# Nyström attention into a mixture of experts on one core: swapped matmul operands, batched copies and a bfloat16 bridge transposed by DMA

## The chip, the cores and the metric

The kernel runs on one core of a Trainium2 chip. The metric is the device time of one execution in microseconds (us), from the profiler's clock. Engines are named as in the profile: PE is TensorE's matmul stream and PEld its weight loads, DVE is VectorE, ACT is ScalarE, POOL is GpSimd, and SP is SyncE, whose queue issues every DMA of this kernel. A tensor in SBUF or PSUM lies on up to 128 partitions.

## The reference, cut to what matters

Attention runs on 64 heads (8 batches by 8 heads) of 576 tokens with 64 features. Means over 18 tokens give 32 landmarks for q and for k. The output is A · Z · C · v, with Z from six steps of a Newton iteration. Its result, read as 4608 tokens of 512 features, goes through a mixture of 8 experts with one expert for each token.

```python
q_lm = q.reshape(B, H, m, S // m, D).mean(axis=3)      # m = 32
k_lm = k.reshape(B, H, m, S // m, D).mean(axis=3)
A = sm(q, k_lm); Bm = sm(q_lm, k_lm); C = sm(q_lm, k)  # softmax of the scaled product
Z = Bm.T / (norm1(Bm) * norminf(Bm) + 1e-06)
for _ in range(6):
    Z = 2 * Z - Z @ Bm @ Z
attn = A @ Z @ C @ v
x = attn.transpose(0, 2, 1, 3).reshape(B * S, H * D)   # 4608 x 512
e_idx = argmax(x @ w_gate); gate_w = softmax(x @ w_gate)[e_idx]; eom = sigmoid(x @ w_output_gate)
out[mask] = gate_w[mask] * eom[mask, e] * (relu(x[mask] @ w1[e]) @ w2[e])
```

## The kernel before, in words

**Attention (L76 to L186).** One unrolled pass for each of the 64 heads. A head's 576 tokens are cut into five chunks, four of 128 and one of 64. The chunks of v, q and k come in by 15 DMAs. PE transposes each q chunk and each k chunk into a PSUM tile `pT` (L90, L96) and DVE copies each out on its own (L91, L97) into `qT` and `kT`, which have the features on partitions. The k chunks are loaded into the buffer of the q chunks, `qS`. Two reductions on DVE give the landmarks `qlmT` (L101) and `klmT` (L103).

The landmark matrix `Bm` is a small matmul (`pBm`, L107), an exponential with its row sum (L110) and a scaling (L112). Its largest column sum comes from a matmul with ones (`pcs`, L115) and a short chain on DVE into `c_bc` (L117 to L119).

The C side is computed with landmarks on partitions: `pC` (L129), 32 by 576, has `qlmT` as the stationary operand and streams `kT`. ACT takes the exponential and the row sums (L131, L135). Then five small transposes `pCT` (L144), five copies `CT` (L146) and five accumulating matmuls `pCv` (L147) give C · v, scaled by the reciprocal row sum at L152.

The Newton chain carries Z · Bm and Z · C · v side by side in one 32 by 96 tile: a first matmul `pWV` (L155), a scaling (L158), and six times a matmul (L161) and a DVE instruction (L162), each of which waits for the one before.

The A side has tokens on partitions. For each of the five chunks there are a matmul `pA` (L169), an exponential with row sum (L172), a reciprocal (L174), a scaling (L175), a transpose `pAT` (L178), a copy `AT` (L180), a matmul `pO` (L182) with the Newton result as the stationary operand, a copy `Ot` (L184) and a DMA into the bridge tensor (L185).

**The bridge.** The attention output lies in DRAM as `x_bridge`, float32, 512 features by 4608 tokens. Four DMAs of 2.36 MB bring it back (`stg`, L203) and four DVE casts (L204) make `xT` in bfloat16, with 128 features on partitions for each of four feature blocks. The DMA of the last block needs the last two heads of every batch.

**The experts (L206 to L305).** A router over 36 token tiles (`plog`, L218, then small DVE work and an exponential and a sigmoid on ACT, L227 and L236), then eight experts of bfloat16 matmuls `ph` (L258) and `py` (L266), then the output.

The kernel is written against a scheduler that places each instruction in its engine's queue when the program is built: an instruction that has its inputs takes a free engine, the one written earlier first. On the chip each queue runs in that order and waits on semaphores. Buffers of a tag are shared in turn: the SBUF tags of attention have two buffers, the PSUM tags one.

Of the kernel before, what the change touches and what calls it, by code (L numbers as in the profile page):

```python
# [34 lines left out]
def kernel(  # L35
# [11 lines left out]
    nc = tc.nc  # L47
    B, H, S, D = q.shape
# [3 lines left out]
    N = B * S  # L52
# [1 line left out]
    E = moe_w_gate.shape[1]  # L54
    F = moe_w1.shape[2]

    x_dram = nc.dram_tensor("x_bridge", (HD, N), F32, kind="Internal").ap()

    with tc.tile_pool(name="attn_const", bufs=1) as cpool, \
         tc.tile_pool(name="attn_sb", bufs=2) as sb, \  # L60
# [13 lines left out]
        while off < S:  # L74
            cp = min(128, S - off)
            tokchunks.append((off, cp))  # L76
            off += cp

        for b in range(B):
            for h in range(H):  # L80
                qT = sb.tile([64, S], F32, tag="qT")
                kT = sb.tile([64, S], F32, tag="kT")
                vS = sb.tile([128, len(tokchunks), 64], F32, tag="vS")
                qS = sb.tile([128, len(tokchunks), 64], F32, tag="qS")
                for ci, (o, cp) in enumerate(tokchunks):
                    nc.sync.dma_start(out=vS[:cp, ci, :], in_=v[b, h, o:o + cp, :])
                    nc.sync.dma_start(out=qS[:cp, ci, :], in_=q[b, h, o:o + cp, :])
                for ci, (o, cp) in enumerate(tokchunks):
                    pT = ps.tile([64, 128], F32, tag="pC")
                    nc.tensor.transpose(pT[:, :cp], in_=qS[:cp, ci, :], identity=I128[:cp, :cp])  # L90
                    nc.vector.tensor_copy(qT[:, o:o + cp], pT[:, :cp])  # L91
                for ci, (o, cp) in enumerate(tokchunks):
                    nc.sync.dma_start(out=qS[:cp, ci, :], in_=k[b, h, o:o + cp, :])
                for ci, (o, cp) in enumerate(tokchunks):
                    pT = ps.tile([64, 128], F32, tag="pC")
                    nc.tensor.transpose(pT[:, :cp], in_=qS[:cp, ci, :], identity=I128[:cp, :cp])  # L96
                    nc.vector.tensor_copy(kT[:, o:o + cp], pT[:, :cp])  # L97
# [23 lines left out]
                Cexp = sb.tile([32, S], F32, tag="Cexp")  # L121
                cs = sb.tile([32, 1], F32, tag="cs")
                cs2 = sb.tile([32, 1], F32, tag="cs2")
                off0 = 0
                first = True
                while off0 < S:
                    w = min(512, S - off0)
                    pC = ps.tile([32, 512], F32, tag="pC")
                    nc.tensor.matmul(pC[:, :w], lhsT=qlmT, rhs=kT[:, off0:off0 + w])  # L129
                    if first:  # L130
                        nc.scalar.activation(out=Cexp[:, off0:off0 + w], in_=pC[:, :w],  # L131
                                             func=EXP, scale=s_c, accum_out=cs)
                        first = False
                    else:
                        nc.scalar.activation(out=Cexp[:, off0:off0 + w], in_=pC[:, :w],  # L135
                                             func=EXP, scale=s_c, accum_out=cs2)
                        nc.vector.tensor_tensor(cs, cs, cs2, op=ADD)
                    off0 += w
                nc.vector.reciprocal(cs, cs)

                pCv = ps.tile([32, 64], F32, tag="pCv")
                for ci, (o, cp) in enumerate(tokchunks):
                    pCT = ps.tile([128, 32], F32, tag="pCT")
                    nc.tensor.transpose(pCT[:cp, :], in_=Cexp[:, o:o + cp], identity=I32)  # L144
                    CT = sb.tile([128, 32], F32, tag="CT")
                    nc.vector.tensor_copy(CT[:cp, :], pCT[:cp, :])  # L146
                    nc.tensor.matmul(pCv, lhsT=CT[:cp, :], rhs=vS[:cp, ci, :],  # L147
                                     start=(ci == 0), stop=(ci == len(tokchunks) - 1))
# [3 lines left out]
                nc.vector.tensor_scalar(out=BmCv[:, 32:96], in0=pCv, scalar1=cs, scalar2=None, op0=MUL)  # L152

                pWV = ps.tile([32, 96], F32, tag="pCv")
                nc.tensor.matmul(pWV, lhsT=Bm, rhs=BmCv)  # L155
                WV = sb.tile([32, 96], F32, tag="WV")
                WV2 = sb.tile([32, 96], F32, tag="WV2")
                nc.vector.tensor_scalar(out=WV, in0=pWV, scalar1=c_bc, scalar2=None, op0=MUL)  # L158
                cur, nxt = WV, WV2
                for _ in range(6):  # L160
                    nc.tensor.matmul(pWV, lhsT=cur[:, :32], rhs=cur)  # L161
# [3 lines left out]
                ZCv = cur[:, 32:96]  # L165

                for ci, (o, cp) in enumerate(tokchunks):
                    pA = ps.tile([128, 32], F32, tag="pA")
                    nc.tensor.matmul(pA[:cp, :], lhsT=qT[:, o:o + cp], rhs=klmT)  # L169
                    Aexp = sb.tile([128, 32], F32, tag="Aexp")  # L170
                    asr = sb.tile([128, 1], F32, tag="asr")
                    nc.scalar.activation(out=Aexp[:cp, :], in_=pA[:cp, :], func=EXP,  # L172
                                         scale=s_a, accum_out=asr[:cp, :])
                    nc.vector.reciprocal(asr[:cp, :], asr[:cp, :])  # L174
                    nc.vector.tensor_scalar(out=Aexp[:cp, :], in0=Aexp[:cp, :],  # L175
                                            scalar1=asr[:cp, :], scalar2=None, op0=MUL)
                    pAT = ps.tile([32, 128], F32, tag="pAT")
                    nc.tensor.transpose(pAT[:, :cp], in_=Aexp[:cp, :], identity=I128[:cp, :cp])  # L178
                    AT = sb.tile([32, 128], F32, tag="AT")
                    nc.vector.tensor_copy(AT[:, :cp], pAT[:, :cp])  # L180
                    pO = ps.tile([64, 128], F32, tag="pO")
                    nc.tensor.matmul(pO[:, :cp], lhsT=ZCv, rhs=AT[:, :cp])  # L182
                    Ot = sb.tile([64, 128], F32, tag="Ot")
                    nc.vector.tensor_copy(Ot[:, :cp], pO[:, :cp])  # L184
                    nc.sync.dma_start(out=x_dram[h * D:(h + 1) * D, b * S + o: b * S + o + cp],  # L185
                                      in_=Ot[:, :cp])  # L186

    TN = 128
    ntiles = N // TN
# [4 lines left out]
    with tc.tile_pool(name="moe_const", bufs=1) as mc, \  # L194
# [2 lines left out]
         tc.tile_pool(name="moe_sb", bufs=2) as msb, \  # L197
         tc.tile_pool(name="moe_ps", bufs=2, space=bass.MemoryType.PSUM) as mps:

        xT = xtp.tile([128, DCH, N], BF16)  # L200
        for dc in range(DCH):
            stg = msb.tile([128, N], F32, tag="stage")
            nc.sync.dma_start(out=stg, in_=x_dram[dc * 128:(dc + 1) * 128, :])  # L203
            nc.vector.tensor_copy(xT[:, dc, :], stg)  # L204

        wg = mc.tile([128, DCH, 2 * E], F32)  # L206
        nc.sync.dma_start(out=wg[:, :, :E], in_=moe_w_gate.rearrange("(dc d) e -> d dc e", d=128))
# [102 lines left out]
```

## Time and profile before

| | |
|---|---|
| time, median of 4 runs | 2439.44 us (2439.1 to 2439.86) |
| the profiled execution, its own time | 2439.67 us |
| its span, first to last instruction | 2437.9 us, 1.8 us less |
| granted TensorE clock, mean | 1.000 |
| PE, PEld busy | 2247.5 us (92%), 1046.3 us (43%) |
| DVE, ACT busy | 1163.6 us (48%), 619.4 us (25%) |
| attention, about | 0 to 1303 us |
| bridge and router, about | 1303 to 1434 us |
| experts and output, about | 1434 to 2438 us |

Busy time counts an engine's instructions alone. A float32 matmul shows as two instructions, each with its own weight load; a transpose shows as one. Since matmuls overlap in the pipeline, the time that one adds to a stream is read from the starts along the chain of waits and not from its duration.

### The profile page before, as it was taken

To read this page: it belongs to the slowest core of one execution; us is meant where nothing else is said; L and a number is where in the kernel's file an instruction comes from. 1 tells how busy PE (TensorE), PEld (TensorE's weight loads), DVE (VectorE), ACT (ScalarE), POOL (GpSimd) and SP (SyncE) were. 2 spreads that over 40 slices of the span, in tenths; PEclk is the share of its full clock that TensorE was granted. 3 is DMA by queue.
4 is the path that set the end of the run, shared out by engine and by line. 5 is a ranking of instruction groups with operands and counts; after the bars stand their busy time and mean duration, and the time that the engine had idled before them with its cause. 6 is when DMAs were issued, how large, how long until landed. Compare 5 with 4: busy or idle time off the path is not lost.

```text
span 2437.9 us, 27936 instructions
## 1 busy us (share of the span) xinstructions
PE 2247.5 (92%) x9267; PEld 1046.3 (43%) x9360; DVE 1163.6 (48%) x4278; ACT 619.4 (25%) x1780; POOL 0.7 (0%) x6
## 2 busy tenths in 40 slices
PE   7999999999999999999993049999999999999999
PEld 3444444444444444444441024444444444444444
DVE  4555555555555555555555422344444535444344
ACT  1111111111111111111113963333333333333333
POOL 0000000000000000000000000000000000000000
PEclk9999999999999999999999999999999999999999
DMA  1111111111111111111225200101010102000012
GB/s 34 31 30 30 30 30 31 31 30 30 31 31 30 30 30 30 30 31 30 66 65 205 85 0 1 70 1 69 1 69 1 69 1 69 1 1 1 1 75 82
DMA packets 171055, 92.08 MB, mean 38 GB/s; under 512 B 137120, under 2 KB 153504, under 8 KB 170400
## 3 DMA queue, kind: packets, MB, share of 16 engines
q1 hardware_dynamic: 170912, 90.30, 12.7%
q8 instruction: 75, 1.23, 0.2%
q14 instruction: 68, 0.56, 0.1%
HBM read 71.34 MB, written 18.87 MB: 37 GB/s over the span
## 4 chain that ended last, share of the span: by engine, by line
PE 86%; DVE 6%; ACT 4%; DMA 2%; issue 1%; SPq 0%; DVEq 0%; ACTq 0%
PE ph L258 20%; PE py L266 20%; PE pO L182 8%; PE pA L169 7%; PE pWV L161 6%; PE pC L129 6%; PE pCv L147 5%; PE pAT L178 4%; PE pCT L144 3%; PE pT L90 3%; PE pT L96 3%; DVE qlmT L101 2%; ACT L236 1%; ACT L227 1%; DVE WV L162 1%; PE pWV L155 1%
## 5 line engine op out<-in xcount | busy, mean ns | idle before, releaser
L258 PE MATMUL ph<-xT,w1b 128*128 128x512 bf16 x2257 | 513.2, 381 | 15.4 <-ACT hT L261 12.6
L261 ACT ACTIVATE hT<-ph 128x512 bf16<-128x512 f32 x576 | 343.7, 597 | 649.7 <-PE ph L258 628.0
L266 PE MATMUL py<-w2b,hT 128*128 128x512 bf16 x2258 | 506.1, 379 | 2.4
L274 DVE TENSOR_SCALAR ysc<-py,coeff 128x512 f32<-128x512 f32 x252 | 189.1, 751 | 451.2 <-PE py L266 434.2
L258 PEld LDWEIGHTS <-w1b 128*128 128x128 bf16 x2304 | 225.7, 98 | 293.6 <-issue 28.7
L266 PEld LDWEIGHTS <-hT 128*128 128x128 bf16 x2304 | 225.4, 98 | 271.8
L161 PE MATMUL pWV<-WV 32*32 32x96 f32 x768 | 200.8, 362 | 30.7 <-DVE WV L162 20.8
L182 PE MATMUL pO<-AT,WV 32*64 32x128 f32 (+1 forms) x640 | 204.9, 421 | 7.1 <-DVE Ot L184 1.3
L172 ACT ACTIVATE Aexp<-pA 128x32 f32<-128x32 f32 (+1 forms) x320 | 62.0, 194 | 518.4 <-PE pAT L178 464.0
L169 PE MATMUL pA<-klmT,qT 64*128 64x32 f32 (+1 forms) x640 | 188.4, 386 | 1.3 <-ACT Aexp L172 0.7
L131 ACT ACTIVATE Cexp<-pC 32x512 f32<-32x512 f32 x64 | 37.5, 586 | 582.4 <-PE pC L129 582.4
L276 DVE TENSOR_TENSOR ytot<-ytot,ysc 128x512 f32<-128x512 f32 x252 | 174.3, 692 | 8.5
L169 PEld LDWEIGHTS pA<-klmT,qT 64*128 64x128 f32 (+1 forms) x640 | 145.5, 286 | 36.8 <-ACT Aexp L172 16.3
L129 PE MATMUL pC<-kT,qlmT 64*32 64x512 f32 (+1 forms) x256 | 149.1, 684 | 0.4 <-DVE kT L97 0.3
L147 PE MATMUL pCv<-vS,CT 128*32 128x64 f32 (+1 forms) x640 | 134.6, 314 | 5.7 <-DVE CT L146 5.7
L146 DVE COPY CT<-pCT 128x32 f32<-128x32 f32 (+1 forms) x320 | 60.1, 188 | 165.4 <-PE pCT L144 165.1
L184 DVE COPY Ot<-pO 64x128 f32<-64x128 f32 (+1 forms) x320 | 83.9, 262 | 106.7 <-PE pO L182 106.2
L90 PE MATMUL pT<-I,qS 128*64 128x128 f32 (+1 forms) x320 | 127.6, 399 | 7.5 <-DMA qS<-in_q_dram 4.9
L96 PE MATMUL pT<-I,qS 128*64 128x128 f32 (+1 forms) x320 | 127.7, 399 | 5.5 <-DMA qS<-in_k_dram 3.9
L182 PEld LDWEIGHTS pO<-AT,WV 32*64 32x64 f32 x640 | 90.5, 199 | 93.5 <-DVE klmT L103 36.6
L162 DVE SCALAR_TENSOR_TENSOR WV<-WV,pWV 32x96 f32<-32x96 f32 x384 | 92.4, 241 | 77.3 <-PE pWV L161 72.8
L161 PEld LDWEIGHTS pWV<-WV 32*32 32x32 f32 x768 | 67.9, 136 | 132.0 <-DVE WV L162 100.1
(66 smaller groups left out, 1541.6 us busy)
## 6 DMA issues: line engine op xcount, KB each, us to landing
w1f<-in_moe_w_dram SPq DMA_DIRECT2D x8, 2048.0 KB, 7.8
w2f<-in_moe_w_dram SPq DMA_DIRECT2D x8, 2048.0 KB, 9.3
stg<-x_bridge SPq DMA_DIRECT2D x4, 2304.0 KB, 9.0
out_dram<-ytot SPq DMA_DIRECT2D x36, 256.0 KB, 2.0
vS<-in_v_dram SPq DMA_DIRECT2D x256, 32.0 KB, 1.9
qS<-in_q_dram SPq DMA_DIRECT2D x256, 32.0 KB, 1.9
qS<-in_k_dram SPq DMA_DIRECT2D x256, 32.0 KB, 1.7
x_bridge<-Ot SPq DMA_DIRECT2D x256, 32.0 KB, 1.8
```

The costliest lines, as they stand in the source:

```text
L90: nc.tensor.transpose(pT[:, :cp], in_=qS[:cp, ci, :], identity=I128[:cp, :cp])
L96: nc.tensor.transpose(pT[:, :cp], in_=qS[:cp, ci, :], identity=I128[:cp, :cp])
L129: nc.tensor.matmul(pC[:, :w], lhsT=qlmT, rhs=kT[:, off0:off0 + w])
L147: nc.tensor.matmul(pCv, lhsT=CT[:cp, :], rhs=vS[:cp, ci, :], start=(ci == 0), stop=(ci == len(tokchunks) - 1))
L161: nc.tensor.matmul(pWV, lhsT=cur[:, :32], rhs=cur)
L169: nc.tensor.matmul(pA[:cp, :], lhsT=qT[:, o:o + cp], rhs=klmT)
L182: nc.tensor.matmul(pO[:, :cp], lhsT=ZCv, rhs=AT[:, :cp])
L258: nc.tensor.matmul(ph, lhsT=w1b[:, dc, fc * 128:(fc + 1) * 128], rhs=xT[:, dc, t0 * TN:t0 * TN + ntk], start=(dc == 0), stop=(dc == DCH - 1))
L261: nc.scalar.activation(out=hT[:, fc, :], in_=ph, func=RELU)
L266: nc.tensor.matmul(py, lhsT=hT[:, fc, tt * TN:(tt + 1) * TN], rhs=w2b[:, fc, :], start=(fc == 0), stop=(fc == FCH - 1))
L274: nc.vector.tensor_scalar(out=ysc, in0=py, scalar1=coeff[:, t, e:e + 1], scalar2=None, op0=MUL)
L276: nc.vector.tensor_tensor(ytot[:, t, :], ytot[:, t, :], ysc, op=ADD)
```

## The change

**Bridge tensor.** `x_bridge` becomes bfloat16, 4608 tokens by 512 features. Each head writes its five chunks as 128 (or 64) tokens of 64 features, 128 bytes for each token. `xT` is allocated ahead of attention and is filled by four DMAs that transpose on the way. The float32 staging and its casts are gone. Two one-column copies out of the last block of `xT` into the two buffers of the tag `stage` stand ahead of the weight loads that use that tag.

**Transposes.** Four chunks are transposed into one PSUM tile of 64 by 512 and copied out at once, the fifth on its own; `pT` has two buffers. k has a buffer `kS` of its own. Edges in program order place the first six transposes of a head (its five of q and the first of k) behind the six Newton matmuls of the head before, one behind each.

**C side.** `pCe` has tokens on partitions: five matmuls with a chunk of `kT` as the stationary operand and `qlmT` streamed, then two exponentials. The transposes `pCT` and the copies `CT` are gone. v has a 65th column of ones, so that `pCv` gives the row sums too.

**A side.** `pAe` has landmarks on partitions: `klmT` is the stationary operand and `qT` is streamed, 512 and 64 columns, with an exponential behind each. `pO2` has a chunk of `AexpT` as the stationary operand and streams the Newton result with a column of ones, so that the division by the row sum comes at the end, on the whole tile. The transposes `pAT` and copies `AT` are gone.

```diff
-    x_dram = nc.dram_tensor("x_bridge", (HD, N), F32, kind="Internal").ap()
+    x_dram = nc.dram_tensor("x_bridge", (N, HD), BF16, kind="Internal").ap()
+    xtp0 = ctx.enter_context(tc.tile_pool(name="xt_early", bufs=1))
+    xT = xtp0.tile([128, HD // 128, N], BF16)
...
+        steps = []
         for b in range(B):
             for h in range(H):
+                prev, steps, nt = steps, [], 0
-                vS = sb.tile([128, len(tokchunks), 64], F32, tag="vS")
+                vSx = sb.tile([128, len(tokchunks), 65], F32, tag="vSx")
+                nc.vector.memset(vSx[:, :, 64:65], 1.0)
+                kS = sb.tile([128, len(tokchunks), 64], F32, tag="kS")
...
+                for c0, c1, w in ((0, 4, 512), (4, 5, 64)):
+                    pT = ps.tile([64, 512], F32, tag="pT", bufs=2)
+                    for ci in range(c0, c1):
+                        o, cp = tokchunks[ci]
+                        tr = nc.tensor.transpose(pT[:, o - c0 * 128:o - c0 * 128 + cp], in_=qS[:cp, ci, :], identity=I128[:cp, :cp])
+                        if prev and 0 <= nt - 0 < 6:
+                            tc.add_manual_dep(tr.ins, prev[nt - 0].ins.name, mybir.DependencyInfo(
+                                mybir.DependencyClass.NoSync, mybir.DependencyReason.DATA), reason="fill the Newton gap")
+                        nt += 1
+                    nc.vector.tensor_copy(qT[:, c0 * 128:c0 * 128 + w], pT[:, :w])
...
-                    pC = ps.tile([32, 512], F32, tag="pC")
-                    nc.tensor.matmul(pC[:, :w], lhsT=qlmT, rhs=kT[:, off0:off0 + w])
...
-                    nc.tensor.transpose(pCT[:cp, :], in_=Cexp[:, o:o + cp], identity=I32)
-                    nc.vector.tensor_copy(CT[:cp, :], pCT[:cp, :])
-                    nc.tensor.matmul(pCv, lhsT=CT[:cp, :], rhs=vS[:cp, ci, :],
...
+                for ci, (o, cp) in enumerate(tokchunks):
+                    nc.tensor.matmul(pCe[:cp, ci * 32:ci * 32 + 32], lhsT=kT[:, o:o + cp], rhs=qlmT)
+                nc.scalar.activation(out=CexpT[:, :128], in_=pCe[:, :128], func=EXP, scale=s_c)
+                nc.scalar.activation(out=CexpT[:64, 128:160], in_=pCe[:64, 128:160], func=EXP, scale=s_c)
+                for ci, (o, cp) in enumerate(tokchunks):
+                    nc.tensor.matmul(pCv, lhsT=CexpT[:cp, ci * 32:ci * 32 + 32], rhs=vSx[:cp, ci, :],
+                                     start=(ci == 0), stop=(ci == len(tokchunks) - 1))
                 cs = sb.tile([32, 1], F32, tag="cs")
+                nc.vector.reciprocal(cs, pCv[:, 64:65])
...
+                    steps.append(nc.tensor.matmul(pWV, lhsT=cur[:, :32], rhs=cur))
...
+                nc.vector.tensor_copy(ZCvx[:, :64], cur[:, 32:96])
+                nc.vector.memset(ZCvx[:, 64:65], 1.0)
+                AexpT = sb.tile([32, S], F32, tag="AexpT")
+                for o, w in ((0, 512), (512, S - 512)):
+                    pAe = ps.tile([32, 512], F32, tag="pAe")
+                    nc.tensor.matmul(pAe[:, :w], lhsT=klmT, rhs=qT[:, o:o + w])
+                    nc.scalar.activation(out=AexpT[:, o:o + w], in_=pAe[:, :w], func=EXP, scale=s_a)
+                pO2 = ps.tile([128, len(tokchunks), 65], F32, tag="pO2")
+                for ci, (o, cp) in enumerate(tokchunks):
+                    nc.tensor.matmul(pO2[:cp, ci, :], lhsT=AexpT[:, o:o + cp], rhs=ZCvx)
+                rinv = sb.tile([128, len(tokchunks), 1], F32, tag="rinv")
+                Ot = sb.tile([128, len(tokchunks), 64], BF16, tag="Ot")
+                for n, c0, c1 in ((128, 0, 4), (64, 4, 5)):
+                    nc.vector.reciprocal(rinv[:n, c0:c1, :], pO2[:n, c0:c1, 64:65])
+                    nc.vector.tensor_tensor(Ot[:n, c0:c1, :], pO2[:n, c0:c1, :64],
+                                            rinv[:n, c0:c1, :].to_broadcast([n, c1 - c0, 64]), op=MUL)
+                for ci, (o, cp) in enumerate(tokchunks):
+                    nc.sync.dma_start(out=x_dram[b * S + o: b * S + o + cp, h * D:(h + 1) * D],
+                                      in_=Ot[:cp, ci, :])
...
-        xT = xtp.tile([128, DCH, N], BF16)
         for dc in range(DCH):
-            stg = msb.tile([128, N], F32, tag="stage")
-            nc.sync.dma_start(out=stg, in_=x_dram[dc * 128:(dc + 1) * 128, :])
-            nc.vector.tensor_copy(xT[:, dc, :], stg)
+            nc.sync.dma_start(out=xT[:, dc, :], in_=x_dram[:, dc * 128:(dc + 1) * 128],
+                              transpose=True)
+        for _ in range(2):
+            hold = msb.tile([128, N], F32, tag="stage")
+            nc.vector.tensor_copy(hold[:, :1], xT[:, DCH - 1, :1])
```

The k transposes are written like the q transposes, out of `kS` into `kT`, and count `nt` on from 5.

## Rows read from the trace of the kernel before

**Rows 1.** Busy time by stretch: us, PE, PEld, DVE, ACT, POOL, clock, DMA share, GB/s.

```profile
300.00:600.00 300.00, 290.15 (x1080) 137.77 (x1080) 160.04 (x795) 38.73 (x240) 0.00 (x0) 1.00 0.13 30
...
1350.00:1400.00 50.00, 4.07 (x64) 2.95 (x64) 19.74 (x144) 49.08 (x81) 0.00 (x0) 1.00 0.11 42
...
1500.00:2000.00 500.00, 497.54 (x2265) 225.84 (x2310) 211.99 (x278) 171.94 (x288) 0.00 (x0) 1.00 0.09 34
```

**Rows 2.** The scaling L158, once a head: duration ns min/median/max, first and last start.

```profile
L158 DVE TENSOR_SCALAR WV<-pWV,c_bc x64: 299/305/306, 25.6 to 1290.1; 32x96 f32<-32x96 f32 x64
```

**Rows 3.** The chain of waits, 611 to 620 us: start us, us, what.

```profile
611.20 0.51 PE pWV L161 x2
611.71 0.35 PE pT L96
...
613.78 0.33 PE pAT L178
614.11 0.24 PE pT L96
614.35 0.61 PE pO L182 x2
...
615.17 1.84 PE pC L129 x2
...
617.12 0.56 PE pA L169 x2
...
618.29 0.35 PE pC L129 x2
618.64 0.24 PE pCT L144
...
619.44 0.35 PE pCv L147 x2
```

**Rows 4.** The chain of waits from the last head's Newton steps to the first expert.

```profile
1292.75 0.25 DVE WV L162
...
1293.05 0.54 PE pWV L161 x2
...
1301.84 1.70 DMA x_bridge<-Ot
...
1308.72 11.91 DMA stg<-x_bridge
...
1323.24 9.93 DMA w2f<-in_moe_w_dram
...
1433.77 0.49 ACT hT L261
```

**Rows 5.** ACT lines, 1270 to 1450 us: count, busy us, mean ns, idle before.

```profile
L236 ACT ACT_TABLE_LOAD x36 | 46.2, 1283 | 0.6
L227 ACT ACT_TABLE_LOAD x35 | 44.9, 1283 | 0.6
```

**Rows 6.** Lines by form, 300 to 600 us: busy us, mean ns, idle before, releasers.

```profile
L97 DVE COPY kT<-pT 64x128 f32<-64x128 f32 x60 | 16.7, 279 | 4.4
...
L131 ACT ACTIVATE Cexp<-pC 32x512 f32<-32x512 f32 x15 | 8.8, 586 | 136.9 <-PE pC L129 136.9
...
L152 DVE TENSOR_SCALAR BmCv<-pCv,cs 32x64 f32<-32x64 f32 x15 | 4.1, 272 | 7.5 <-PE pCv L147 6.8
...
L97 DVE COPY kT<-pT 64x64 f32<-64x64 f32 x15 | 3.2, 212 | 0.0
```

**Rows 7.** DMA: queue packets, MB, share of 16 engines; an issue with KB and landing us.

```profile
q1 hardware_dynamic: 170912, 90.30, 12.7%
...
stg<-x_bridge SPq DMA_DIRECT2D x4, 2304.0 KB, 9.0
```

**Rows 8.** The first head on the timeline: v and k loads, last k transpose.

```profile
7.78 0.43 SPq L86 DMA_DIRECT2D vS<-in_v_dram  x1
...
14.28 0.31 PE L96 MATMUL pT<-I,qS 64*64 64x64 f32 x1 [0.38 <-DVE kT L97]
```

More of the change, by code (lines that the diff above doesn't have):

```diff
@@ L85 @@
                 for ci, (o, cp) in enumerate(tokchunks):
-                    nc.sync.dma_start(out=vS[:cp, ci, :], in_=v[b, h, o:o + cp, :])
+                    nc.sync.dma_start(out=vSx[:cp, ci, :64], in_=v[b, h, o:o + cp, :])
                     nc.sync.dma_start(out=qS[:cp, ci, :], in_=q[b, h, o:o + cp, :])
-                for ci, (o, cp) in enumerate(tokchunks):
-                    pT = ps.tile([64, 128], F32, tag="pC")
-                    nc.tensor.transpose(pT[:, :cp], in_=qS[:cp, ci, :], identity=I128[:cp, :cp])
-                    nc.vector.tensor_copy(qT[:, o:o + cp], pT[:, :cp])
@@ L92 @@
[L92 to L97, printed above, removed]
+                for c0, c1, w in ((0, 4, 512), (4, 5, 64)):
[8 more added lines that the diff above has]
+                    nc.vector.tensor_copy(qT[:, c0 * 128:c0 * 128 + w], pT[:, :w])
@@ new lines @@
+                for ci, (o, cp) in enumerate(tokchunks):
+                    nc.sync.dma_start(out=kS[:cp, ci, :], in_=k[b, h, o:o + cp, :])
+                for c0, c1, w in ((0, 4, 512), (4, 5, 64)):
+                    pT = ps.tile([64, 512], F32, tag="pT", bufs=2)
+                    for ci in range(c0, c1):
+                        o, cp = tokchunks[ci]
+                        tr = nc.tensor.transpose(pT[:, o - c0 * 128:o - c0 * 128 + cp], in_=kS[:cp, ci, :], identity=I128[:cp, :cp])
+                        if prev and 0 <= nt - 0 < 6:
+                            tc.add_manual_dep(tr.ins, prev[nt - 0].ins.name, mybir.DependencyInfo(
+                                mybir.DependencyClass.NoSync, mybir.DependencyReason.DATA), reason="fill the Newton gap")
+                        nt += 1
+                    nc.vector.tensor_copy(kT[:, c0 * 128:c0 * 128 + w], pT[:, :w])
@@ L119 @@
                 nc.vector.reciprocal(c_bc, c_bc)
-                Cexp = sb.tile([32, S], F32, tag="Cexp")
-                cs = sb.tile([32, 1], F32, tag="cs")
[L123 to L127, printed above, removed]
-                    pC = ps.tile([32, 512], F32, tag="pC")
-                    nc.tensor.matmul(pC[:, :w], lhsT=qlmT, rhs=kT[:, off0:off0 + w])
[L130 to L143, printed above, removed]
-                    nc.tensor.transpose(pCT[:cp, :], in_=Cexp[:, o:o + cp], identity=I32)
-                    CT = sb.tile([128, 32], F32, tag="CT")
-                    nc.vector.tensor_copy(CT[:cp, :], pCT[:cp, :])
-                    nc.tensor.matmul(pCv, lhsT=CT[:cp, :], rhs=vS[:cp, ci, :],
-                                     start=(ci == 0), stop=(ci == len(tokchunks) - 1))
+                pCv = ps.tile([32, 65], F32, tag="pCv")
@@ new lines @@
+                pCe = ps.tile([128, 160], F32, tag="pCe")
+                CexpT = sb.tile([128, 160], F32, tag="CexpT")
+                for ci, (o, cp) in enumerate(tokchunks):
[5 more added lines that the diff above has]
+                                     start=(ci == 0), stop=(ci == len(tokchunks) - 1))
@@ L150 @@
+                cs = sb.tile([32, 1], F32, tag="cs")
+                nc.vector.reciprocal(cs, pCv[:, 64:65])
                 BmCv = sb.tile([32, 96], F32, tag="BmCv")
                 nc.vector.tensor_copy(BmCv[:, :32], Bm)
-                nc.vector.tensor_scalar(out=BmCv[:, 32:96], in0=pCv, scalar1=cs, scalar2=None, op0=MUL)
-                pWV = ps.tile([32, 96], F32, tag="pCv")
+                nc.vector.tensor_scalar(out=BmCv[:, 32:96], in0=pCv[:, :64], scalar1=cs, scalar2=None, op0=MUL)
@@ L155 @@
+                pWV = ps.tile([32, 96], F32, tag="pWV")
                 nc.tensor.matmul(pWV, lhsT=Bm, rhs=BmCv)
@@ L160 @@
                 for _ in range(6):
-                    nc.tensor.matmul(pWV, lhsT=cur[:, :32], rhs=cur)
+                    steps.append(nc.tensor.matmul(pWV, lhsT=cur[:, :32], rhs=cur))
                     nc.vector.scalar_tensor_tensor(out=nxt, in0=cur, scalar=2.0, in1=pWV,
@@ L164 @@
                     cur, nxt = nxt, cur
-                ZCv = cur[:, 32:96]
-                for ci, (o, cp) in enumerate(tokchunks):
[L168 to L186, printed above, removed]
@@ new lines @@
+                ZCvx = sb.tile([32, 65], F32, tag="ZCvx")
+                nc.vector.tensor_copy(ZCvx[:, :64], cur[:, 32:96])
[5 more added lines that the diff above has]
+                    nc.scalar.activation(out=AexpT[:, o:o + w], in_=pAe[:, :w], func=EXP, scale=s_a)
```

## The prediction, made before the changed kernel ran

> **What bounds the kernel now.** I read the table of stretches first. In attention PE is busy for 290 of 300 us, in the experts for 497.5 of 500, and in the router for 4 of 50, where ACT has 49 [rows 1]. The change touches only attention and the bridge, so the reader should look at what PE is busy with there. The granted clock is 1.00 in all three stretches, the router with its idle PE included; I count no change of clock.
>
> The scaling L158 runs once a head and gives the period: (1290.1 − 25.6)/63 = 20.07 us [rows 2]. Next is the chain of waits. It runs almost wholly through PE, matmul after matmul with no gap, apart from the Newton steps, where PE and DVE alternate [rows 3, 4]. So a head costs what its matmuls occupy of PE, and a little idle.
>
> The same chain at the end of attention gives the bridge: the last write lands at 1303.5, the last staging DMA and the last cast follow, and the router can start at 1323.2 [rows 4]. From there to the first expert at 1433.8 ACT swaps function tables, 71 loads of 1.28 us, 91 of 110 us [rows 4, 5]. The change leaves that as it is, and the experts behind it.
>
> **Pricing PE.** Starts along the chain give the time that an instruction adds. One of pC occupies 1.84/2 = 0.92 us for 32 stationary and 512 streamed columns, one of pA 0.56/2 = 0.28 for 128 and 32 [rows 3]. The line through the two is 1.667 ns for each column, loaded or streamed, plus 13 ns. It gives 0.333 for a transpose (64 and 128; the row has 0.35) and 0.173 for one of pCv (32 and 64; 0.175) [rows 3]. So a loaded column costs as much as a streamed one, which matters because the change swaps the operands. The Trainium skill says otherwise (TensorE: Matmul & The Clock Gate, Step-by-step: what each phase is for): the next tile's weights load while the present matmul runs. pA disagrees, since its 32 streamed columns alone would take 0.07 us and not 0.28.
>
> **PE's work, by head.** Removed:
> - pC 1.84 + 0.35 = 2.19, and pCT 4 × 0.24 + 0.17 = 1.13
> - pA 4 × 0.56 + 0.35 = 2.59 (the last chunk by the line)
> - pAT 4 × 0.33 + 0.17 = 1.49, and pO 4 × 0.61 + 0.45 = 2.89 (last chunks by the line)
>
> That is 10.29 us. Added:
> - pCe, with pA's shape: 2.59
> - pAe, with pC's shape: 2.19
> - pO2, 128 loaded and 65 streamed columns: 2 × 0.335 = 0.67, the last chunk 0.46, together 3.14
>
> That is 7.92. Kept: ten transposes 8 × 0.35 + 2 × 0.24 = 3.28, pCv 1.75 (the 65th column adds 2 ns), the two small matmuls 0.24 each by the line, and seven of pWV at 2 × 0.226. Sum 8.68. PE's work falls from 18.97 to 16.60 us. Before, 20.07 − 18.97 = 1.10 us of a period were idle.
>
> **The chain through a period.** PE won't be as full as before, since the edges tie the transposes to the Newton steps and less work is left to fill the waits. I follow one period from the end of a head's sixth Newton matmul:
> - PE takes two k transposes (0.70) while DVE does the last Newton instruction (0.25) and the copy of the result (about 0.2, as the 64-wide copy in [rows 6]).
> - pO2 of the old head then has its input and was written earlier, so it goes first: 3.84. Three k transposes: 4.78.
> - The batched copy. 128 columns take 279 ns and 64 take 212 [rows 6], so 512 take about 0.68. It starts behind the fourth transpose at 4.54 and ends at 5.26; PE has nothing to do for 0.5 us.
> - pCe with the two small matmuls slipped in, 3.07: 8.37. The reduction for klmT and the chains for Bm and c_bc lie beside it on DVE and ACT.
> - The exponential, under the 0.59 us of a 512-wide one [rows 6], about 0.3. pAe is the only thing ready and can't be interrupted: 10.2.
> - pCv: 11.96. Reciprocal, scaling (0.27, [rows 6]) and handovers 0.5, first pWV 0.54, scaling 0.3 (its row, [rows 2]): 13.35.
> - Six Newton steps. Matmul, DVE and handovers make 0.86 [rows 4], so 5 × 0.86 + 0.54 = 4.84: 18.2. A transpose of q fits in each gap, as one of k does now [rows 3].
>
> A period of **18.2 us** has 1.6 of idle PE. The bounds are 16.6 (no idle) and 20.07 (the waits eat the gain). DVE loses work (35 copies, reciprocals and scalings of a head's chunks become 8), so it won't bind. I take 17.2 to 19.0 as the likely band. Periods: 63 × (18.2 − 20.07) = **−118 us**.
>
> **Start.** k no longer waits for the q transposes to free a buffer. The fifteenth load of the kernel is issued at 7.78 and is one of the next head's [rows 8]; it will be the first head's last of k, landed two us later, so the last k transpose comes near 9.9 and not at 14.28 [rows 8]. From there the steps above (13.35 + 0.3 − 4.78 to the end of the scaling) put the first L158 near 18.5, and not 25.6: **−7 us**.
>
> **Bridge.** From the last write's landing to the router's start there are now 19.7 us [rows 4]. In the new kernel the first three blocks' transposing DMAs can run while later heads still compute; each holds only the loads behind it in SP's queue, and those are prefetches for a later head. The last block follows the last write. No row shows a transposing DMA. From below: it moves 1.18 MB, half of a staging DMA of 9.0 us, so 4.5 us [rows 7]. From above: queue q1's packets take 0.127 × 16 × 2437.9 us / 170912 = 29 ns on average [rows 7], 4608 packets of 256 bytes over 16 engines 8.4 us, with the 1.7 of a landing [rows 4] about 10. I take 6.5, nearer to the staging DMA, which moves the same tensor: **−13 us** (−9.7 to −15.2). The weight loads wait for the short copies behind the last block, 10 us and a cast later than they could go; the router's 110 us cover that several times. The last head's own tail stays near 13 us: pO2 in one run and five writes take the place of five rounds of pO and Ot.
>
> **Sum.** 2439.67 (this execution's own time, within 0.3 us of the runs' median) − 118 − 7 − 13 = **2302 us**.
>
> **The rivals.**
> - PE stays as full as before or fuller, because the fills fit better than my order has them: a period of 16.6 to 17.2, −219 to −181, and −20 for the rest: 2201 to 2239. For it: before, idle was only 1.10. Against: pO2 stands between the k transposes and everything that depends on them. 14 in 100.
> - The waits grow: pAe falls into a Newton gap, the batched copy sits ahead of a Newton instruction on DVE, and the edges keep transposes from filling other holes. A period of 19.0 to 20.0: 2352 to 2415. For it: one uninterruptible pAe is 1.84 us. 13 in 100.
> - All four transposing DMAs wait for the last write, since each reads a column range of rows that every head writes into. The tail is then 4 × 6.5 to 4 × 10 and not 6.5: 2321 to 2336. For it: writes and reads interleave in address. Against: the ranges share no byte. 11 in 100.
> - Weights load beside the stream after all. Then pCe costs 5 × 0.13 and pO2 5 × 0.24, 3.9 us less, a period near 14.3 and a time near 2056. pA speaks against it [rows 3]. 2 in 100. (It is the rule of the Trainium skill, TensorE: Matmul & The Clock Gate, given above; the trace doesn't bear it out.)
> - **Slower:** the transposing DMA moves single two-byte elements. 589,824 a block at 29 ns over 16 engines are 1069 us [rows 7], and the time over 3300. It decides from the point where the exposed transposes take more than the 125 us of the attention gain plus today's 19.7, so 36 us a block if all four are exposed, 145 if one is. Against: the change asks for a transpose as a form of DMA and not for a strided read. 6 in 100. The Trainium skill (DMA: Bandwidth & Descriptors, Rules for kernel authors) puts a factor of 19 between a hardware transpose and a plain DMA with a rearranged access pattern; no run here shows either.
> - The gain is eaten wholly, within 0.2% (what a measurement of this kernel can tell from no change): 1 in 100.
>
> **How the numbers follow.** The forecast's own band, a period of 17.2 to 19.0, is 2239 to 2352 with 53 in 100. The range 2222 to 2385 adds the nearer halves of the two neighbours and the serial bridge; outside are some 8 below with the 2 of the hidden weights, some 6 above, and the 7 at or over today's time. Faster by over 0.2%: 53 + 14 + 13 + 11 + 2 = 93; within: 1; slower: 6.
>
> **What would show it.** The distance between starts of the scaling in the Newton chain gives the period: 18.2. The chain of waits should show pO2 as one run of about 3.1 us ahead of the last k transposes, 0.5 us of PE idle at the batched copy, pAe ahead of pCv, and no idle over 0.5 us elsewhere. pO2's pairs should stand 0.67 apart; 0.24 would mean hidden weights. Three transposing DMAs should be issued before the last head ends and the fourth land in 5 to 10 us. The router's 110 us and the experts' 1004 us should be what they are. I am wrong if the period is a wait's and not PE's: a DVE copy, a load, or SP's queue.

## The result, and the profile after

Eight runs of the changed kernel have a median of 2176.52 us (2175.55 to 2177.39), twelve of the kernel before 2439.06 (2438.66 to 2439.86): a ratio of 0.8923 (0.8914 to 0.8932). It is faster, as forecast, but by 263 us and not by 138; 2176.5 lies 45 us below the low end of the range.

The table of stretches, with the columns of [rows 1]:

```profile
300.00:600.00 300.00, 273.73 (x1137) 151.10 (x1136) 124.89 (x513) 25.76 (x108) 0.00 (x0) 1.00 0.16 32
1100.00:1150.00 50.00, 6.51 (x73) 3.76 (x72) 20.25 (x150) 49.09 (x82) 0.00 (x0) 1.00 0.12 44
```

PE is still what attention is busy with, ACT still what the router is busy with, and the clock is 1.00 in both. The scaling, now L161, gives the period as in [rows 2]:

```profile
L161 DVE TENSOR_SCALAR WV<-pWV,c_bc x64: 305/305/306, 17.2 to 1049.5; 32x96 f32<-32x96 f32 x64
```

(1049.5 − 17.2)/63 = 16.385 us, where 18.2 was forecast and 20.072 stood before. The 264.0 us between the two spans (2437.9 and 2173.9) are:

| | before | after | difference | forecast |
|---|---|---|---|---|
| first scaling | 25.6 | 17.2 | −8.4 | −7 |
| 63 periods | 1264.5 | 1032.3 | −232.2 | −118 |
| last scaling to the router's first copy | 33.4 | 19.5 | −13.9 | −13 |
| the router | 110.3 | 103.3 | −7.0 | 0 |
| experts and output | 1004.1 | 1001.6 | −2.5 | 0 |

The chain of waits (start, us, what) through one period, from the end of a head's sixth Newton matmul to the same point a head later, and below it the end of attention. It answers to [rows 3, 4].

```profile
612.65 0.78 PE pT L111 x3
613.43 2.35 PE pO L179 x10
615.79 0.37 PE pT L111
616.18 0.69 DVE kT L116
616.91 2.27 PE pCe L144 x10
619.27 0.29 ACT CexpT L145
619.60 1.08 PE pCv L148 x8
620.67 0.24 PE pBm L126 x2
620.92 0.22 PE pCv L148 x2
621.14 1.71 PE pAe L175 x2
622.84 0.26 PE pcs L134 x2
623.12 0.19 DVE c_bc L136
...
623.77 0.32 DVE WV L161
624.13 0.52 PE pWV L164 x2
624.65 0.35 PE pT L99
...
628.50 0.52 PE pWV L164 x2
629.03 0.78 PE pT L111 x3
...
1062.22 6.48 DMA xT<-x_bridge
...
1172.36 0.49 ACT hT L264
```

Read the counts beside the times. Ten matmuls of `pO` in a row (the line's name for the tile `pO2`) take 2.35 us, so 0.47 a pair, where the forecast had 0.67. Ten of `pCe` take 2.27. Eight of the ten load 128 columns and stream few (65 and 32). In the single records these eight start 0.213 us apart, after the first two of the run, and 128 × 1.667 ns = 0.213 us: the load sets the pace, and the streamed columns cost nothing beside it. The two of `pAe` (512 streamed) take 1.71, or 0.853 each: here the stream sets it, and the load of 32 columns is free. The last two of `pCv` (65 streamed) take 0.22, again the stream's time. By contrast a lone transpose of q between two Newton matmuls still takes 0.35, as in [rows 3]; three transposes of k in a row take 0.78.

### The profile page after: what moved, and what is told of

It is laid out like the page before. It is cut to its first block, busy times and chain, and to the rows that moved or that the text cites. A ratio compares the mean times of both kernels' runs of the same rounds, so it can differ in the third digit from the quotient of the medians.

```text
span 2173.9 us, 23658 instructions
## 1 busy us (share of the span) xinstructions
PE 1962.4 (90%) x8626; PEld 984.2 (45%) x8720; DVE 904.1 (42%) x2676; ACT 537.0 (25%) x1134; POOL 0.7 (0%) x6
## 4 chain that ended last, share of the span: by engine, by line
PE 83%; DVE 7%; ACT 4%; DMA 2%; issue 2%; SPq 1%; DVEq 0%; ACTq 0%
PE ph L261 23%; PE py L269 22%; PE pWV L164 7%; PE pO L179 7%; PE pCe L144 7%; PE pAe L175 5%; PE pCv L148 4%; PE pT L99 4%; PE pT L111 3%; DVE kT L116 2%; DVE qT L104 2%; ACT L239 1%; ACT L230 1%; DMA w2f<-in_moe_w_dram 1%; DVE WV L161 1%
## 5 line engine op out<-in xcount | busy, mean ns | idle before, releaser
L144 PE MATMUL pCe<-qlmT,kT 64*128 64x32 f32 (+1 forms) x640 | 145.5, 380 | 33.9 <-DVE kT L116 33.9
L175 PE MATMUL pAe<-qT,klmT 64*32 64x512 f32 (+1 forms) x256 | 149.0, 684 | 10.4 <-ACT AexpT L176 10.4
L144 PEld LDWEIGHTS pCe<-qlmT,kT 64*128 64x128 f32 (+1 forms) x640 | 132.2, 300 | 50.4 <-DVE kT L116 45.9
L179 PE MATMUL pO<-ZCvx,AexpT 32*128 32x65 f32 (+1 forms) x640 | 151.5, 403 | 0.6 <-DVE ZCvx L169 0.6
L179 PEld LDWEIGHTS pO<-ZCvx,AexpT 32*128 32x128 f32 (+1 forms) x640 | 131.6, 297 | 34.8 <-DVE ZCvx L170 26.0
L99 PE MATMUL pT<-I,qS 128*64 128x128 f32 (+1 forms) x320 | 127.7, 399 | 5.5 <-DMA qS<-in_q_dram 5.5
L148 PE MATMUL pCv<-vSx,CexpT 128*32 128x65 f32 (+1 forms) x640 | 95.2, 313 | 25.2 <-ACT CexpT L145 25.2
L111 PE MATMUL pT<-I,kS 128*64 128x128 f32 (+1 forms) x320 | 96.4, 399 | 0.7 <-DMA kS<-in_k_dram 0.5
L176 ACT ACTIVATE AexpT<-pAe 32x512 f32<-32x512 f32 (+1 forms) x128 | 51.2, 400 | 144.3 <-PE pAe L175 144.3
L183 DVE RECIPROCAL rinv<-pO 128x4 f32<-128x4 f32 (+1 forms) x128 | 21.3, 166 | 157.1 <-PE pO L179 157.1
```

The lines of the kernel that those rows point to most:

```text
L99: tr = nc.tensor.transpose(pT[:, o - c0 * 128:o - c0 * 128 + cp], in_=qS[:cp, ci, :], identity=I128[:cp, :cp])
L111: tr = nc.tensor.transpose(pT[:, o - c0 * 128:o - c0 * 128 + cp], in_=kS[:cp, ci, :], identity=I128[:cp, :cp])
L144: nc.tensor.matmul(pCe[:cp, ci * 32:ci * 32 + 32], lhsT=kT[:, o:o + cp], rhs=qlmT)
L148: nc.tensor.matmul(pCv, lhsT=CexpT[:cp, ci * 32:ci * 32 + 32], rhs=vSx[:cp, ci, :], start=(ci == 0), stop=(ci == len(tokchunks) - 1))
L175: nc.tensor.matmul(pAe[:, :w], lhsT=klmT, rhs=qT[:, o:o + w])
L179: nc.tensor.matmul(pO2[:cp, ci, :], lhsT=AexpT[:, o:o + cp], rhs=ZCvx)
```

## The experiments

**Theory.** Within a run of matmuls whose stationary operands have the same rows and columns, the next load hides behind the stream before it, and one costs the larger of the two, at 1.667 ns a column. Where the shape changes, the load isn't hidden and about 0.13 us are added. Before, nearly every pair stood between pairs of other shapes, so the rows that the price was made from all held such a change. Rivals: the additive price stands and something else got cheaper; or what breaks a run is a wait on a semaphore and not a shape.

**Three more matmuls, once in one run and once between the pairs.** The two kernels do the same extra work: three matmuls of 32 by 32 into columns that are added to `pO2` (97 and not 65 for a chunk) and that nothing reads.

```diff
 # e_switch_once
+for ci in range(3):
+    nc.tensor.matmul(pO2[:32, ci, 65:97], lhsT=ZCvx[:, :32], rhs=ZCvx[:, :32])
 for ci, (o, cp) in enumerate(tokchunks):
     nc.tensor.matmul(pO2[:cp, ci, :65], lhsT=AexpT[:, o:o + cp], rhs=ZCvx)
 # e_switch_between
 for ci, (o, cp) in enumerate(tokchunks):
     nc.tensor.matmul(pO2[:cp, ci, :65], lhsT=AexpT[:, o:o + cp], rhs=ZCvx)
+    if ci < 3:
+        nc.tensor.matmul(pO2[:32, ci, 65:97], lhsT=ZCvx[:, :32], rhs=ZCvx[:, :32])
```

> Three extra matmuls of 32 rows by 32 columns stand in one run ahead of pO2 in each head; their results go to unused columns. Shape theory (a weight load hides behind the stream before it only where both stationary operands have the same rows by columns): one more change of shape and 6 x 0.053 us, about +0.65 us a head, 2218 us. Additive theory (loaded and streamed columns always add, the price of the prediction): 3 x 0.24 = 0.72 us a head, 2222. Wait theory (a load is late only where its instruction waits on a semaphore; these have no wait of their own): 6 x 0.053 = 0.32 us a head, 2197. The run is the base for the next one.

> The same three extra matmuls, one behind each of the first three pairs of pO2 and not in one run ahead of them. No instruction is added and no wait. Shape theory: two changes of shape for each, in which neither pO2's stream (0.108) nor the extra one's loads are hidden and some 0.13 us pass, so about 0.9 to 1.1 us a head over the run with all three ahead, 60 to 70 us more, and pO2's pairs no longer 0.43 us apart. Additive theory and wait theory: no difference between the two runs.

The kernel with the three in one run took 2186.54 us, with a period of 16.534, and the one with the same three between the pairs 2238.79, with 17.360. Order alone costs 0.826 us a head, 52 us in all, somewhat less than the 60 to 70 that the theory of shapes had. The timelines (start, us, engine, line, what, form, count), first in one run, then between:

```profile
619.49 0.52 PE L179 MATMUL pO<-ZCvx 32*32 32x32 f32 x6
619.94 2.37 PE L181 MATMUL pO<-ZCvx,AexpT 32*128 32x65 f32 x10
622.24 0.67 PE L111 MATMUL pT<-I,kS 128*64 128x128 f32 x2
```

```profile
614.80 0.68 PE L179 MATMUL pO<-ZCvx,AexpT 32*128 32x65 f32 x2
615.41 0.31 PE L181 MATMUL pO<-ZCvx 32*32 32x32 f32 x2
615.65 0.69 PE L179 MATMUL pO<-ZCvx,AexpT 32*128 32x65 f32 x2
...
617.36 1.09 PE L179 MATMUL pO<-ZCvx,AexpT 32*128 32x65 f32 x4
618.38 0.67 PE L111 MATMUL pT<-I,kS 128*64 128x128 f32 x2
```

By the starts, the sixteen take 622.24 − 619.49 = 2.75 us in the first and 618.38 − 614.80 = 3.58 in the second. A pair and its small pair take 0.85, where by the starts inside the runs they take 0.43 and 0.11. The first order has four changes of shape from the transposes to the transposes, the second nine (the last chunk's 64 columns are a change too): 0.83/5 is 0.17 each. An additive price sees no difference between the two orders, and neither kernel has a wait between these matmuls that the other hasn't.

The run cost only 0.15 us a head on average, less than all three expectations. In 14 of the 42 heads from 200 to 900 us a fourth transpose of k came ahead of `pO2`, and the wait for k's copy went (a period of 15.84). In the others the period is 16.83, 0.45 more than in the changed kernel, which is six small loads of 0.053 and one change of 0.13. The second kernel has the same two kinds of heads, of 16.66 and 17.66, so the comparison of the two orders stands.

**The same three, with the shape of their neighbours.** The insertions again, but the stationary operand is the chunk of `AexpT`, so only the stream is shorter.

```diff
+    if ci < 3:
+        nc.tensor.matmul(pO2[:cp, ci, 65:97], lhsT=AexpT[:, o:o + cp], rhs=ZCvx[:, :32])
```

> The changed kernel with three extra matmuls in pO2's run, one behind each of its first three pairs, as in the run with the small ones between, but with pO2's own stationary operand (32 by 128) and 32 streamed columns, so that they load four times as many columns and the shape stays. Shape theory: the run isn't broken, each extra pair costs its loads alone, 2 x 0.213 us, 1.28 us a head and 2257 us, and the starts in the run stay 0.213 apart. If any instruction between two pairs breaks the run, whatever its shape: 1.28 and the 0.83 us that the small ones lost by standing between, 2310. Additive theory: 3 x 0.56 = 1.68 us a head, 2283.

It took 2238.25 us, with a period of 17.365, below all three figures. The timeline:

```profile
649.42 0.69 PE L179 MATMUL pO<-ZCvx,AexpT 32*128 32x65 f32 x2
649.91 0.57 PE L181 MATMUL pO<-ZCvx,AexpT 32*128 32x32 f32 x2
650.30 0.66 PE L179 MATMUL pO<-ZCvx,AexpT 32*128 32x65 f32 x2
650.76 0.57 PE L181 MATMUL pO<-ZCvx,AexpT 32*128 32x32 f32 x2
651.15 0.66 PE L179 MATMUL pO<-ZCvx,AexpT 32*128 32x65 f32 x2
...
653.00 0.67 PE L111 MATMUL pT<-I,kS 128*64 128x128 f32 x2
```

Sixteen take 3.58 us, 0.22 each, and two pairs 0.88 at the head of the run and 0.85 behind it, where the additive price gives 0.67 + 0.56 = 1.23. Another instruction in between, with another stream, doesn't break the run. It adds six loads of 0.213, 1.28 us. On average the kernel lost 0.98 a head, again because in one head of three four transposes of k came ahead of `pO2`; in the others the period is 17.67, 1.29 more than in the changed kernel. That this kernel and the one before it have the same time is chance, six full loads against three small pairs with five more changes of shape.

Another tile doesn't break a run either. In the changed kernel `pBm`, the last chunk of `pCv` and `pAe` follow each other with the same shape, 64 by 32, and start 0.055 and 0.107 us apart (43 cases each), the stream's time. It is enough that one of the two counts changes: from `pO2`'s chunks of 128 columns to the one of 64, with 32 rows both times, 0.342 us pass and not 0.213.

**Each part alone.** Three kernels take the kernel before and add one part: the C side (`pCe`, the 65th column), the A side with the bridge, or the grouped transposes with their edges. The C side alone also has a PSUM buffer of its own for `pWV`, as the changed kernel has; the transposes alone still share the one buffer of `pC`, where the changed kernel has two for `pT`.

```diff
 # e_c_side: on the kernel before
-    nc.tensor.matmul(pC[:, :w], lhsT=qlmT, rhs=kT[:, off0:off0 + w])
+    nc.tensor.matmul(pCe[:cp, ci * 32:ci * 32 + 32], lhsT=kT[:, o:o + cp], rhs=qlmT)
 # e_a_bridge: on the kernel before
-    nc.tensor.matmul(pA[:cp, :], lhsT=qT[:, o:o + cp], rhs=klmT)
-    nc.tensor.matmul(pO[:, :cp], lhsT=ZCv, rhs=AT[:, :cp])
+    nc.tensor.matmul(pAe[:, :w], lhsT=klmT, rhs=qT[:, o:o + w])
+    nc.tensor.matmul(pO2[:cp, ci, :], lhsT=AexpT[:, o:o + cp], rhs=ZCvx)
 # e_transposes: on the kernel before
-    nc.vector.tensor_copy(kT[:, o:o + cp], pT[:, :cp])
+    nc.vector.tensor_copy(kT[:, c0 * 128:c0 * 128 + w], pT[:, :w])
```

> The kernel before with the C side alone changed (pCe, the 65th column of v). Additive theory: PE loses 2.19 + 1.13 and gains 2.59 us a head, 47 us less, 2392. Shape theory: the run of pCe costs 2.27, pCv in one run of 1.3 and not 1.75, so 1.4 to 1.5 us a head, 2340 to 2350.

> The kernel before with the A side and the bridge changed, the rest as it was. Additive theory: PE loses 2.59 + 1.49 + 2.89 and gains 2.19 + 3.14 us a head, 1.64 x 64 = 105, and 20 to 23 for bridge and router, 2312 us. Shape theory: pO2's run costs 2.35 and pAe's streams 2.06, 2.56 x 64 = 164 and the same 20 to 23, 2253.

> The kernel before with the transposes alone changed: four into one PSUM tile, one copy for four, a buffer of its own for k, the edges. Additive theory: PE's columns stay, no gain, and up to 0.7 us a head lost in the wait for the wide copy, 2440 to 2480. Shape theory: the k transposes come in a run of 0.213 us each and not 0.35, about 0.5 us a head less, against the same wait: 2410 to 2450.

They took 2344.14 us (period 18.533, −1.54 a head), 2280.72 (17.904, −2.17) and 2410.25 (19.668, −0.40). Alone they sum to −4.11 a head, together they give −3.69. The chain of the C side alone, and then that of the A side alone:

```profile
602.54 0.56 PE pCe L126 x2
603.11 0.61 PE pO L167 x2
...
607.78 1.43 PE pCv L130 x10
```

```profile
600.99 1.71 PE pAe L176 x2
602.69 2.30 PE pO L180 x10
...
620.45 2.30 PE pO L180 x10
```

The same `pCe` that takes 0.45 a pair in a run takes 0.56 here, one pair at a time, which is the price of `pA` in [rows 3]. So the C side's time falls in the band of the theory of shapes in part by luck: `pCe` never stood in a run, and with `pCv`'s run (1.43 for 1.75) the terms give 1.05 of the 1.54 us; where the rest comes from stays open. The A side has `pO` in a run of ten in every head, at 2.30, and `pAe` at 1.71, as the theory of shapes prices them. Its time still lies between the two theories' figures, 0.39 a head short of the larger gain: 0.27 of that is idle PE (0.66 us of a period before, and 0.93 here, where PE is busy for 284.46 of the 300 us from 300 on), and the rest is open.

**The edges.** Both groups of edges, for q and for k, left out.

```diff
-if prev and 0 <= nt - 0 < 6:
-    tc.add_manual_dep(tr.ins, prev[nt - 0].ins.name, mybir.DependencyInfo(
...
```

> The changed kernel without the edges that tie six transposes to the Newton matmuls. If the edges gave the part of the gain that was not forecast (1.8 us a head): 2230 us or more. If they only fix an order that comes about anyway, since a transpose of q has nothing else to fill: within 15 us of 2176, with at most one q transpose of a head in another hole.

It took 2211.7 us, with a period of 16.917, 0.53 a head worse, which is between the two figures. Three Newton gaps of a head stayed empty (0.33 us of idle PE each), and k's copy stood behind the divisions `Ot` on DVE.

**k's transposes ahead of `pO2`.** One more edge.

```diff
+if prev:  # first_o: the old head's first pO2 matmul, tr: the last k transpose
+    tc.add_manual_dep(first_o.ins, tr.ins.name, mybir.DependencyInfo(
...
```

> The changed kernel with one more edge: pO2 of a head stands behind all five k transposes of the next head and not between them. If the k transposes, their copy (0.69 us, in which PE idles 0.76 us a head now) and pCe are the chain that sets the period: the copy goes under pO2's 2.35 us, the idle and one change of shape go away, 0.8 to 1.0 us a head, 2115 to 2125 us. If a period is set elsewhere (DVE, DMA, SP's queue): no change, 2176.

It took 2158.6 us, with a period of 16.109. The chain:

```profile
619.56 1.23 PE pT L111 x5
620.79 2.30 PE pO L182 x10
623.09 2.21 PE pCe L147 x10
```

The copy is hidden: `pCe` starts when `pO2` ends, and the 0.76 us in which the chain stood off PE are gone. Only 0.28 of them came back. A transpose of q fell behind the sixth Newton matmul (0.24), and `pBm` now cuts `pCv`'s run after its first pair: the pieces take 1.80 us where 1.54 stood. The chain for c_bc still begins behind `pAe`.

**The small matmuls first.** In addition `pBm` goes ahead of `pCe` and `pcs` ahead of `pCv`.

```diff
+# mC: the first pCe matmul, mV: the first pCv matmul
+tc.add_manual_dep(mC.ins, mBm.ins.name, mybir.DependencyInfo(
...
+tc.add_manual_dep(mV.ins, mcs.ins.name, mybir.DependencyInfo(
...
```

> The kernel with all k transposes first, and two more edges: the small matmul pBm ahead of pCe and pcs ahead of pCv. If what k_first gave back lies in pBm standing in the middle of pCv's run (0.24 us) and in the c_bc chain behind pAe (0.66 us in which PE idles): 15.6 to 15.8 us a head and not 16.1, 2130 to 2140. If the idle only moves behind pCv, where the scaling of C v is waited for: no change, 2159.

It took 2148.73 us, with a period of 15.908, between the two figures. The timeline:

```profile
620.14 1.91 PE L184 MATMUL pAe<-qT,klmT 64*32 64x512 f32 x2
622.21 1.43 PE L154 MATMUL pCv<-vSx,CexpT 128*32 128x65 f32 x10
624.25 0.52 PE L167 MATMUL pWV<-BmCv,Bm 32*32 32x96 f32 x2 [0.39 <-DVE BmCv L164]
```

Now `pAe` stands in the exponential's wait, the order that the prediction had, and what is waited for behind `pCv` is the scaling of C · v and no longer c_bc.

**The two one-column copies left out.**

```diff
-for _ in range(2):
-    hold = msb.tile([128, N], F32, tag="stage")
-    nc.vector.tensor_copy(hold[:, :1], xT[:, DCH - 1, :1])
```

> The changed kernel without the two one-column copies ahead of the weight loads. The weights may load during attention. If the six function table loads that the router lost (70 before, 64 after, 7 us) come from the order of DVE's work around the copies and the weight casts, their count changes and with it the router's 104 us, by up to 10 us either way; otherwise 2176 within 3 us.

It took 2191.83 us, 15.3 more, at the same period (16.393). From the last scaling to the router 25.3 us pass and not 19.5, the router takes 110.7 and not 103.3, and the experts 1004.0 and not 1001.6. The timeline of SP's queue without the copies, and then with them:

```profile
1062.62 0.50 SPq L242 DMA_DIRECT2D w1f<-in_moe_w_dram  x1
1063.31 9.76 SPq L203 DMA_TRANSPOSE xT<-x_bridge  x1
```

```profile
1033.90 4.63 SPq L203 DMA_TRANSPOSE xT<-x_bridge  x1
1045.40 9.93 SPq L203 DMA_TRANSPOSE xT<-x_bridge  x2
1058.43 2.38 SPq L187 DMA_DIRECT2D x_bridge<-Ot  x5
1062.22 4.35 SPq L203 DMA_TRANSPOSE xT<-x_bridge  x1
```

Without them a weight load of 2 MB is issued 0.7 us ahead of the last transposing DMA, which then holds SP for 9.76 us and not 4.35. The router's part shows in ACT's lines over the whole execution, without the copies and with them:

```profile
L235 ACT ACT_TABLE_LOAD x36 | 46.2, 1283 | 0.6
L226 ACT ACT_TABLE_LOAD x35 | 44.9, 1283 | 1.1 <-DVE es L225 0.3
```

```profile
L239 ACT ACT_TABLE_LOAD x33 | 42.3, 1283 | 0.6
L230 ACT ACT_TABLE_LOAD x32 | 41.1, 1283 | 0.6
```

With the copies ACT's queue has some exponentials in pairs and some sigmoids in pairs, and 65 table loads stand on the two lines, where 71 stood in [rows 5] and stand again without them. Six loads of 1.283 us are 7.7 us; the router lost 7.0 against the kernel before, and 7.4 against this one. The other runs agree: each of the eight kernels with the copies and the old router has 65, and each of the four without the copies 71.

**A version that beats both.** The edges of the kernel above, and the router in two passes: the exponentials of all 36 tiles, then one sigmoid over all of them.

```diff
-            nc.scalar.activation(out=eom, in_=lg[:, E:], func=SIG)
+        nc.scalar.activation(out=eomall, in_=lgall[:, :, E:], func=SIG)
```

> The kernel of the run before with the router regrouped: the logits of all 36 tiles are kept, the exponentials run tile by tile, and one sigmoid over all tiles follows, the same computation with two function table loads in place of some 64. If the table loads are what the router takes its 103 us for, 64 x 1.28 = 82 us go, less what DVE's own 60 us of work over 36 tiles then bounds: 40 to 60 us less, 2075 to 2095. If DVE or the weights bound it at once: 20 us less or none.

It took 2076.65 us (2076.5 to 2077.24, four runs), 0.8515 of the time before (0.85 to 0.8531) and 72 us less than the kernel above. Three table loads are left in the whole kernel. From the router's first copy to the experts behind it 31.5 us pass, where 103.3 did. The one sigmoid also merges 36 products of mask and sigmoid on DVE into one. The table of stretches for it:

```profile
1042.00:1067.00 25.00, 7.75 (x124) 5.63 (x123) 22.48 (x226) 9.43 (x63) 0.00 (x0) 1.00 0.43 164
```

DVE, 22.5 of 25 us busy, is now what the router waits for: ACT waits 15.1 of these 25 us for DVE's input to the exponential.

## Why the prediction was right or wrong

**What bounds the kernel** was right: PE's matmuls in attention, ACT's table loads in the router.

**Pricing PE is the step that failed**, in "a loaded column costs as much as a streamed one". The runs showed in its place the larger of the two, and 0.13 to 0.17 us for each change of shape. `pA` is 2 × 0.213 + 0.13 = 0.56 and `pC` 2 × 0.853 + 0.13 = 1.84, the same two numbers that the additive line was drawn through. The two rows that the line was then tested on can't tell the prices apart: a transpose is 0.333 by the line and 0.213 + 0.13 = 0.34 by the new price, with 0.35 in its row, and a pair of `pCv` is 0.35 by the line and 0.34 by the new price, with 0.35 in its row. `pO` (64 loaded, 128 streamed) is 0.67 by the line, 0.56 by the new price, and 0.61 in [rows 3], so it speaks for neither. What could have told them apart was in the same trace. The second instruction of a pair always has its neighbour's shape, and in the records of the kernel before it starts 0.855 us after the first for `pC`, 0.107 for `pCv` and 0.162 for `pWV`, where the line gives 0.920, 0.173 and 0.226.

The new price isn't exact either: it is 0.05 short for `pO`, and gives 0.35 for `pCT`, whose row has 0.24. In the records from 200 to 900 us the shape changes between neighbouring matmuls 1526 times before and 939 times after, 44 and 22 in a period. The 22 that went would be 2.9 of the 3.69 us that a head gained, at 0.13 each; this is an estimate, since part of a change can lie in a wait.

The Trainium skill (TensorE: Matmul & The Clock Gate, Step-by-step: what each phase is for) has the next tile's weights load while the present matmul runs. Dismissed on `pA`'s row, it holds within runs of one shape: where the shape stays and nothing is waited for, the next load starts a median of 27 ns after the matmul before it starts (1499 cases), and where a chunk of `pCT` follows one of `pCv` in the kernel before, 242 ns (140 cases). The trace before bore it out too, with the same 27 ns in 862 cases. The rival made from it (2056 us) was too low, because it priced streams alone, and `pO` and `pCe` are set by their loads: `pO2`'s pairs stand 0.43 apart, neither the line's 0.67 nor the 0.24 that the prediction took as the sign of hidden weights. The Trainium skill (TensorEngine Tiling (Array Packing), Key Properties) also says that a change of tiling mode drains the engine. It gives no time; the 0.13 us fit it, but that this is the mechanism no run here shows.

**The chain through a period**, by its steps, in us:

| from the sixth Newton matmul | forecast | measured |
|---|---|---|
| k transposes, `pO2`, the batched copy | 5.26 | 4.26 |
| `pCe` (forecast with `pBm` and `pcs`) | 3.11 | 2.27 |
| exponential, `pCv`, `pAe` (measured with `pBm`) | 3.59 | 3.66 |
| to the end of the scaling (measured with `pcs`) | 1.39 | 1.25 |
| six Newton steps | 4.84 | 4.94 |
| period | 18.2 | 16.38 |

Its order was nearly right: three transposes of k came ahead of `pO2` and not two, and `pAe` fell behind `pCv`, which laid the exponential's wait (0.42) and the chain for c_bc (1.03 with the scaling) open. Term by term PE was priced too high: `pO2` took 2.35 for 3.14, `pCv` 1.30 for 1.75, `pCe` 2.27 for 2.59, four transposes of k 1.15 for 1.40, `pAe`'s first pair 1.71 for 1.84. That is 1.94 us, and the period came out 1.8 below the forecast.

The waits were about right in sum. The chain stands off PE for 3.1 us of a period, but in part of that PE works beside it, on the first `pWV`, `pAe`'s second pair, the fifth Newton matmul and the last transpose of q. The table of stretches shows 26.27 of 300 us without PE, 1.43 of a period, and 1.6 were forecast. (The same table gives 0.66 before, where the prediction had 1.10, so it may count some 0.4 too little.) The longest idle times of PE are 0.53 at the copy and 0.43 at the exponential, so the sentence that no idle over 0.5 us would be found elsewhere held.

**Start and bridge** were right in mechanism. The last k transpose of the first head starts at 9.78, near the 9.9 forecast. Three transposing DMAs were issued ahead of the last head's writes, and the last landed 6.48 us after its issue, where 6.5 was taken. From the write's landing on, the bridge gave −13.2 for −13. That it is so near is luck in part: 6.5 was picked between 4.5 and 10, and the four DMAs took 6.5 to 8.1. The serial bridge and the strided transpose didn't come.

**The router and the experts** were to stay as they were. The router lost 7.0 us, through the order of ACT's queue that the two small copies changed, which the prediction mentioned for the weights alone. The 2.5 us of the experts go with the copies too: without them the experts take 1004.0 again. With them one `hT` of the first expert stands among the router's work in ACT's queue, at 1099.62; how that gives 2.5 us no run shows.

**The edges**, which the prediction took for a tie that leaves holes, are worth 35 us.

## What to carry to other kernels

Before pricing a matmul from a row, look at its neighbours: a pair that stands alone between other shapes carries the change of shape, and the same instruction in a run does not. Test a line through two rows on others at which a rival price gives another figure, before it prices a change. Grouping instructions by stationary shape (and ACT's functions by table) can be worth more than removing some of them.

## What the runs showed that was not expected

- The order of otherwise equal matmuls moved 52 us of 2187: five more changes of shape a head, 0.83 us.
- A transposing DMA of 1.18 MB held SP's queue for 4.35 us, and for 9.76 when a 2 MB load had been issued 0.7 us ahead of it.
- Two copies of one column on DVE, 0.15 us each, took six table loads off ACT and 15 us off the time.
- In five of the eleven experiments the granted clock fell in the router alone. In the kernel with three matmuls of the neighbours' shape it was 0.56 on average from 1140 to 1230 us, so mostly at the lower level, 1.2 GHz. PE had been busy all through attention before it, and was busy for 13.6 of those 90 us. The profiled execution of the changed kernel kept 1.00 in its router. The time didn't show it: the router took 103.2 us there and 103.3 here, since ACT sets it. Other executions differ in the same way: four of the changed kernel's eight runs have a mean clock of 0.979 or 0.98 over the span and took 2175.55 to 2177.39 us, and the four with 1.00 took 2175.71 to 2176.7. Two runs of the kernel before that stood beside the experiment have 0.979 too.
